# One rotation table, two q and k buffers, one tail transpose, and the second token block's input made during attention: a fused attention and two-layer feed-forward kernel

## The chip, the cores and the metric

One Trainium2 chip, one core. The metric is the device time of one execution in microseconds (us). Each kernel was run several times; the median counts. One more execution was taken by the hardware profiler, and every duration below is from that one.

## The reference, cut to what matters

Attention over 4 batches x 8 heads, 576 tokens, head width 64, in float32, then two feed-forward layers over all 2304 tokens (512 -> 2048 -> 512):

```python
q_rot, k_rot = rotate(q), rotate(k)                 # x1*cos - x2*sin, x1*sin + x2*cos
scores = 1/sqrt(64) * q_rot @ k_rot.T
attn = exp(scores - max); attn /= attn.sum + 1e-9
x = (attn @ v) as [2304, 512]
x = (h - tanh(h)) @ w_out    with h = x @ w_in       # layer one
x = (h * sigmoid(1.702 h)) @ w_out2, h = x @ w_in2   # layer two
```

float32 accuracy is kept by splitting every operand into a high part (rounded to the matmul's format) and a low part (the rest) and adding three products.

## The kernel before, in words

**Work and stages.** Attention works on 16 pairs of heads (`pairs`, 4 batches x 4 pairs). The feed-forward part ("MoE" in the names) works on 6 blocks of 384 tokens x 16 slices of 128 hidden columns x 2 layers: 192 items. An item is an "up" product of 12 matmuls (`up`, L702), an activation on ACT and DVE (`act`), a split on ACT and POOL (`split`, L799 and L801) and a "down" product (`down`, L816).

**A pair in attention.** SP loads q and k of pair n with a swapped copy (`load_qk`, L335; tile `qk`, three buffers). POOL rotates them: two multiplications by the table `tab` (`rope`, L356) and an addition (L358), each over 128x1152 values; ACT rounds the high part (`qk_hi`, L362), POOL takes the low part (`qk_lo`, L400). Four DMAs lay k out twice (`k_twin`, L408, tile `kt`, two buffers) and four lay out q (`q_pair`, L411). Pair 0 goes another way: its q and k come in four pieces with their piece of the table (`load_first`, L341 and L342) and are rotated on DVE (`first_rope`, L372). `v` is split by `v_hi` and `v_lo` (L419). The table holds the q half scaled by 1/8 and the k half unscaled: `tab` is [128, 2, 2, 576].

There are nine units of scores (`UNITS`): four blocks of 128 queries for each head, and one unit (2, 4) that holds the last 64 queries ("tail") of both heads in one 128-row tile. For each unit PE makes scores (L435), DVE the row maximum (L441), ACT the exponentials (L447). PE then transposes the exponentials (`etrans`: L465 the tail unit against the first 512 keys, L472 the others, L476 the last 64 keys of two query blocks, L479 the last 64 keys of one head's tail as a 64x64 transpose with a 64x64 identity, once per head). `evac` copies each transposed bank: ACT the high part (L503), DVE the low part (L501). `pv` multiplies with v (L517); `pv_out` copies to `xt` (L526, L528), `save` writes it to DRAM (L532). Group 1 (`eh`, `el` with 640 columns) holds, per head, 256 query columns and that head's 64 tail columns: head 0 at 0 to 319, head 1 at 320 to 639. Row sums go through `r_add` to `r_save` (one small transpose a pair, L542).

**Feed-forward input.** `x_fetch` (L724, L727) brings a 128-row slice of a block and the reciprocal row sums back from DRAM; `x_split` adds, scales and splits it: three POOL operations (L738, L740, L744) and one ACT copy (L742) for each of four slices. Block 0's tiles live in the pool `xp`, which is open from the start. Block 1's live in the pool `mx`, which is opened only by `close_early`, after the last exponentials (the plan's token `early`). Blocks 0 and 1 go through the first four weight slices one after the other, then the next four and so on (`cuts`). Four weight slices are converted during attention; the other twelve of layer one afterwards, 24 halves of two DVE operations (L282, L284), two POOL (L280, L293) and two ACT operations (L271, L289) each.

**What sets the order.** Every step is an `Op` with a priority, engine costs, what it reads and writes and the buffers it holds. `Plan.order` is a list scheduler in the kernel's own source: it simulates engines and buffers with the hand-written costs, picks among ready operations by priority (`OFF` in units of us from a pair's start, `PER` a pair's length, `T(i)` for items), and its result is fixed as the program order of each engine. So on PE, ACT, DVE, POOL and the SP queue everything runs in that order, and an operation that waits holds up what is behind it. `CAPS` says how many buffers of each tile there are, `XA` and `XB` from what planned time on blocks 0 and 1 may be fetched, `T1` where the items start, and the term 8.6 or 6.3 in `item_ops` how late a "down" stands behind its "up".

Of the kernel before, what the change touches and what calls it, by code (L numbers as in the profile page):

```python
# [40 lines left out]
XA, XB = 218.7, 271.2  # L41
LOOK = {"DVE": 0.15, "ACT": 0.15, "POOL": 0.6, "PE": 0.1, "SP": 2.0}
CAPS = {"qk": 3, "kt": 2, "v": 2, "vw": 2, "e": 7, "ehs": 2, "els": 2, "ehx": 1, "elx": 1, "xt": 3, "mx": 4,
        "sum": 2, "rw": 2, "sp": 2, "st": 2, "cz": 2, "wpa": 4, "wpb": 12, "x": 2, "rb": 1, "rc": 2, "xb0": 1,
        "xb1": 1, "part": 2, "y": 4, "z": 2, "w": 2, "t": 2, "mk": 2, "gh": 2, "gl": 2}

CS, CP, X1 = -0.5, 13.2, 8
CT = (41.4, 75, 90, 105, 120, 135, 150, 159.7)
G = (19.0, 24.0, 17.0)

# [146 lines left out]
def attention_moe_kernel(ctx: ExitStack, tc, qk, v, w1_in, w1_out, w2_in, w2_out, rope_tab, eye, out):  # L197
# [114 lines left out]
    tab = a1.tile([128, 2, 2, S], F32, name="tab")  # L312
# [18 lines left out]
    def load_qk(n, j):  # L331
        b, hp = pairs[n]
        if ("qk", n) not in st:
            st["qk", n] = ae.tile([128, 2, 2, S], F32, tag="qk", name="qk", bufs=3)
        nc.sync.dma_start(out=st["qk", n][:, :, j], in_=qk[b, hp, :, :, j])  # L335

    def load_first(j, c0, c1):
        if ("qk", 0) not in st:
            st["qk", 0] = ae.tile([128, 2, 2, S], F32, tag="qk", name="qk", bufs=3)
# [26 lines left out]
    def first_rope(part, j, c0, c1):  # L366
# [3 lines left out]
        if part < 2:  # L370
            z = (x, y)[part]
            eng.tensor_mul(z, z, tab[:, part, j, c0:c1])  # L372
# [85 lines left out]
    def etrans(n, blk, kk):  # L458
# [14 lines left out]
        else:  # L473
# [3 lines left out]
            if c0 == 2:  # L477
                r = slice(64 * h, 64 * h + 64)
                nc.tensor.transpose(p[0:64, 256:320], st["e", n, (2, 4)][r, 512:576], ident[r, r])  # L479
        st["pe", n, blk, kk] = p  # L480

    def evac(n, blk, kk, low):
# [4 lines left out]
        if c0 == 4:  # L487
            def view(t):
                return t.rearrange("p k (h q) -> p k h q", h=2)[:, 0:4, :, 256:320]
            src, hi, lo = p.rearrange("p k (h q) -> p k h q", h=2), view(eh), view(el)  # L490
        else:
            off = 320 * h if g == 1 else 0
# [3 lines left out]
            else:  # L496
                wd = 320 if c0 == 2 else 256
# [22 lines left out]
    def pv_out(n, h, part):  # L520
        cols, wd = (slice(256, 576), 320) if part == 1 else (slice(0, 256), 256)
        if ("x", n, h) not in st:
            st["x", n, h] = ap.tile([128, S], F32, tag="xt", name="xt", bufs=3)
# [20 lines left out]
    def r_copy(n):  # L544
        rw = st["rw", n] = ap.tile([9, 128], F32, tag="rw", name="rw")
# [20 lines left out]
    for m, a in enumerate(cuts0):  # L566
# [4 lines left out]
        op(-9e3 + m * 20, lambda a=a: load_first(*a), [("SP", 1.26, 1.5 * w)], (), [("q0", m), ("tab", m)], [("qk", 0)], nd=2,  # L571
           dl=(1.9, 0.8 - LAG["SP"]))
    for m, a in enumerate(cuts0):
# [3 lines left out]
        for p in range(2):  # L577
            op(pr + p, lambda p=p, a=a: first_rope(p, *a), [_cost("DVE", d)],
               [("q0", m), ("tab", m)], [("q0", m, p)], [("qk", 0)], port=True)
# [12 lines left out]
    for n in range(NP):  # L592
# [10 lines left out]
        if n:  # L603
            for j in (1, 0):
                op(at("ld") - j * 0.1, bind(load_qk, j), [("SP", 0.62, 1.5)], (), [("qj", n, j)], [Q], G[0] if n == 2 else G[1] if n == 3 else 0.0, dl=HBM)
            for p in range(2):
                op(at(f"r{p}"), bind(rope, p), [_cost("POOL", 2.66)] + alt,
                   [("qj", n, 0), ("qj", n, 1)] + [("tab", m) for m in range(4)], [("rp", n, p)], [Q], port=True)
# [32 lines left out]
        for b, (blk, kk) in enumerate(BLK):  # L641
# [5 lines left out]
            else:  # L647
                us = [IX[h, c0], IX[h, c0 + 1]] + ([IX[2, 4]] if c0 == 2 else [])
                cost, wd = (("PE", 0.6, 0.75), 320) if c0 == 2 else (("PE", 0.25, 0.4), 256)
# [6 lines left out]
            op(at(f"t{b}") + 0.6, bind(evac, blk, kk, False), [_cost("ACT", {512: 0.59, 320: 0.42, 256: 0.37}[wd])],  # L656
               [("t", n, b)], [("th", n, b)], [bt] + ge)
            op(at(f"t{b}") + 1.2, bind(evac, blk, kk, True), [_cost("DVE", {512: 0.683, 320: 0.48, 256: 0.42}[wd])],
               [("t", n, b), ("th", n, b)], [("tl", n, b)], [bt] + ge)
        bi = {x: b for b, x in enumerate(BLK)}  # L660
        for h in range(2):
            for part in range(2):
# [6 lines left out]
                for stage in range(3):  # L669
                    need = [(x, n, bi[blk, stage]) for x in ("th", "tl")]  # L670
                    if part and stage < 2:
                        need += [(x, n, bi[(2, 4), 0]) for x in ("th", "tl")]
# [9 lines left out]
            op(at(f"pv{h}0") + 2, bind(save, h), [("SP", 0.5, 0.78)], [("xt", n, h, 0), ("xt", n, h, 1)], [("xs", n, h)],  # L682
               [("xt", n, h)], dl=(1.2, 0.8))
# [31 lines left out]
    def x_fetch(mo, j, kk):  # L715
# [6 lines left out]
        rb = (pools["mx"] if j else xp).tile([128, TB], F32, tag="rb", name="rb", bufs=2 if j else 1)  # L722
# [113 lines left out]
    T1 = PER * NP + 12  # L836
# [4 lines left out]
    def fetch_ops(mo, j, t, after=0.0):  # L841
        X = (f"xb{j % 2}", mo, j)
        gate = ["early"] if j % 2 else []
        for kk in range(NK):
# [4 lines left out]
            else:  # L849
                bs = {b for b, *_ in pieces(j)}  # L850
                ns = [b * HP + kk for b in bs]
                rb = ("rc" if j else "rb", mo, j, kk)
# [162 lines left out]
```

## Time and profile before, and how to read it

| what | value |
|---|---|
| median of 3 runs | 1111.84 us (1110.89 to 1112.17) |
| the profiled execution | 1112.36 us |
| its span in the profile | 1110.6 us |
| attention | 0 to about 291 us |
| layer one with weight conversion | about 289 to 420 us |
| the rest of both layers | 420 to 1107 us |
| granted TensorE clock | 1.00 in all 40 slices |

PE is the matmul engine, PEld its weight load, DVE, ACT and POOL the vector, scalar and general engines, SP the engine whose queue issues all DMAs here ("SPq" is that queue). L435 is line 435. A row such as "L479 PE ... x32" tells of 32 instructions of that line. In a timeline a bracket says how long the engine had idled before the instruction and what ended the wait. Matmuls are pipelined: a busy time of 0.28 us can stand for 0.12 us of progress, so costs on PE are read from start to start.

### The profile page before, as it was taken

Reading aid. Unit: us, or ns where it says so; the run is one execution under the profiler, and the core shown is the slowest. Engines: PE = TensorE matmul, PEld = TensorE weight load, DVE = VectorE, ACT = ScalarE, POOL = GpSimd, SP = SyncE. Lnnn points to the kernel's source line nnn. Section 1 sums busy time; section 2 is a strip of 40 time slices with the busy share of each in tenths; the row PEclk is TensorE's granted clock in tenths of the full one; section 3 lists DMA queues with packets and bytes.
Section 4 is the critical chain, followed back from the end, with each engine's and each line's share of the span. In section 5 each row is a group of like instructions: output and inputs, shape, how many; then the busy total and the mean of one; then the engine's idle time right before and its main releaser. Section 6 shows DMA issues by size and latency. Waiting matters only on the chain.

```text
span 1110.6 us, 17746 instructions
## 1 busy us (share of the span) xinstructions
PE 1075.9 (97%) x6296; PEld 1008.8 (91%) x6296; DVE 651.8 (59%) x1168; ACT 668.4 (60%) x1474; POOL 597.7 (54%) x502
## 2 busy tenths in 40 slices
PE   4999999999999999999999999999999999999998
PEld 4898999898889989999999999988899999999997
DVE  5999999989769997666667679544212111111110
ACT  4999999988768776556566587654322232232222
POOL 3988888973466667436263267767423232332222
PEclk9999999999999999999999999999999999999999
DMA  9688687764434315203022034443101010010000
GB/s 321 231 295 300 226 302 252 263 220 158 117 124 130 114 58 155 74 1 114 1 79 83 15 101 129 156 133 114 57 1 58 1 57 1 2 42 1 29 1 29
DMA packets 76969, 126.22 MB, mean 114 GB/s; under 512 B 7248, under 2 KB 44368, under 8 KB 76880
## 3 DMA queue, kind: packets, MB, share of 16 engines
q1 hardware_dynamic: 76880, 125.08, 34.2%
q8 instruction: 50, 0.82, 0.3%
q14 instruction: 39, 0.32, 0.1%
HBM read 77.79 MB, written 18.95 MB: 87 GB/s over the span
## 4 chain that ended last, share of the span: by engine, by line
PE 66%; DVE 13%; POOL 6%; ACT 6%; issue 6%; DMA 1%; SPq 1%; POOLq 0%; DVEq 0%; ACTq 0%
PE y L816 27%; PE ps_h L702 27%; PE sp L435 4%; PE ps_o L517 4%; DVE mx L441 3%; PE ps_e L472 3%; DVE el L501 3%; POOL w L293 2%; POOL gl L801 2%; DVE cz L282 2%; DVE cz L284 2%; ACT e L447 2%; POOL cz L280 1%; ACT eh L503 1%; DVE eh L501 1%
## 5 line engine op out<-in xcount | busy, mean ns | idle before, releaser
L702 PE MATMUL ps_h<-xh,w 128*128 128x384 f32 x1536 | 421.2, 336 | 0.6 <-DVE xt L526 0.5
L801 POOL TENSOR_TENSOR gl<-t,gh 128x384 fp32r<-128x384 f32 x192 | 194.7, 1015 | 361.6 <-ACT gh L799 356.8
L702 PEld LDWEIGHTS ps_h<-xh,w 128*128 128x128 f32 x1536 | 280.3, 188 | 5.8 <-DVE t L786 1.1
L702 PE MATMUL ps_h<-xl,w 128*128 128x384 f32 x768 | 257.3, 335 | 0.0
L769 DVE TENSOR_TENSOR t<-t,ps_h 128x384 f32<-128x384 f32 x96 | 53.1, 553 | 280.5 <-ACT t L767 280.5
L816 PE MATMUL y<-gh,w 128*128 128x384 f32 x768 | 195.4, 335 | 2.0 <-ACT gh L799 2.0
L799 ACT CAST gh<-t 128x384 fp32r<-128x384 f32 x192 | 98.8, 514 | 151.1 <-DVE t L792 82.6
L816 PE MATMUL y<-w,gh 128*128 128x512 f32 x576 | 179.4, 392 | 0.0
L767 ACT ACTIVATE t<-ps_h 128x384 f32<-128x384 f32 x96 | 47.1, 491 | 189.1 <-PE ps_h L702 185.7
L702 PEld LDWEIGHTS ps_h<-xl,w 128*128 128x128 f32 x768 | 144.2, 188 | 3.8
L816 PEld LDWEIGHTS y<-gh,w 128*128 128x128 f32 x768 | 138.4, 188 | 3.6 <-ACT gh L799 3.3
L816 PE MATMUL y<-gl,w 128*128 128x384 f32 x384 | 129.2, 337 | 5.3 <-POOL gl L801 5.3
L816 PEld LDWEIGHTS y<-w,gh 128*128 128x128 f32 x576 | 106.7, 188 | 18.2 <-ACT part L825 0.6
L435 PE MATMUL sp<-kt,qt 128*128 128x288 f32 x624 | 115.0, 312 | 2.8 <-ACT e L447 2.5
L816 PE MATMUL y<-w,gl 128*128 128x512 f32 x288 | 114.3, 397 | 1.6 <-POOL gl L801 1.6
L447 ACT ACTIVATE e<-sp,mx 128x576 f32<-128x576 f32 x144 | 107.0, 746 | 14.3 <-DVE mx L441 13.1
L441 DVE TENSOR_REDUCE mx<-sp 128x1 f32<-128x576 f32 x144 | 106.8, 748 | 10.1 <-PE sp L435 9.4
L503 ACT CAST eh<-ps_e 128x512 fp32r<-128x512 f32 (+2 forms) x208 | 102.7, 528 | 8.6 <-PE ps_e L472 6.1
L293 POOL TENSOR_TENSOR w<-cz,w 128x512 fp32r<-128x512 f32 x64 | 82.8, 1294 | 45.6 <-ACT w L289 44.8
L784 DVE SCALAR_TENSOR_TENSOR w<-z,ps_h 128x384 f32<-128x384 f32 x96 | 52.8, 550 | 78.0 <-ACT t L777 76.6
L501 DVE TENSOR_TENSOR el<-ps_e,eh 128x512 fp32r<-128x512 f32 x144 | 95.8, 683 | 4.3 <-ACT eh L503 2.5
L435 PEld LDWEIGHTS sp<-kt,qt 128*128 128x128 f32 x624 | 89.2, 191 | 7.0 <-ACT e L447 5.1
(70 smaller groups left out, 1735.4 us busy)
## 6 DMA issues: line engine op xcount, KB each, us to landing
kt<-qk SPq DMA_DIRECT2D x64, 288.0 KB
qk<-in_qk_dram SPq DMA_DIRECT2D x30, 576.0 KB
st<-in_moe_w_in_dram SPq DMA_DIRECT2D x32, 512.0 KB
st<-in_moe_w_out_dram SPq DMA_DIRECT2D x32, 512.0 KB
qt<-qk SPq DMA_DIRECT2D x64, 144.0 KB
xs<-xt SPq DMA_DIRECT2D x32, 288.0 KB
x<-xs SPq DMA_DIRECT2D x16, 384.0 KB
v<-in_v_dram SPq DMA_DIRECT2D x16, 320.0 KB
```

The costliest lines, as they stand in the source:

```text
L293: nc.gpsimd.tensor_sub(w[:, 2 * self.half + 1], self.cz, w[:, 2 * self.half].bitcast(F32))
L435: nc.tensor.matmul(sp[:, half, 0:HS], lhsT=w, rhs=m[:, half * HS:(half + 1) * HS], start=(o == 0), stop=(o == len(ops) - 1))
L441: nc.vector.tensor_reduce(mx, st["sp", n, i], axis=AX.XY, op=ALU.max, negate=True)
L447: nc.scalar.activation(e.rearrange("p (a b) -> p a b", a=2), st.pop(("sp", n, i)), AF.Exp, bias=st.pop(("mx", n, i)), accum_out=st["sum", ...
L501: nc.vector.tensor_sub(lo, src, hi.bitcast(F32))
L503: nc.scalar.copy(hi, src)
L702: nc.tensor.matmul(p, lhsT=wi[:, a, kk, :], rhs=xx[:, kk, :], start=(o == 0), stop=(o == 11))
L769: nc.vector.tensor_mul(gt[i], gt[i], p)
L784: nc.vector.scalar_tensor_tensor(w, z, G_C[3], p, op0=ALU.mult, op1=ALU.mult)
L799: nc.scalar.copy(gs[i][0], g)
L801: nc.gpsimd.tensor_sub(gs[i][1], g, gs[i][0].bitcast(F32))
L816: nc.tensor.matmul(y, lhsT=lhs, rhs=rhs, start=first and o == 0, stop=last and o == 2)
```

## The change

One rotation table, scaled by 64^-0.25 for q and k alike, [128, 2, 576], loaded in two pieces and read by `rope` as a broadcast over q and k. Two `qk` buffers in place of three, one `rw` buffer in place of two. The last 64 keys of both tails are transposed by one 128-row transpose, in the third step of block (0, 2) alone; the 640 columns of group 1 become head 0 (256), both tails (128), head 1 (256), so head 1's product comes out with its tail in front, its `xt` grows to 640 columns and is saved by two DMAs. Block 1's split tiles move to `xp`, lose the `early` gate, and its fetch may start earlier; so may block 0's. Priorities, some planned costs and `MD` (the lag of a "down") are new, so the planner lays out every engine's order anew.

```diff
-    "ld": -29.13, ... "hi": -6.31, "lo": -5.94, "dk": -13.75,
+    "ld": -35.69, ... "hi": -6.57, "lo": -7.13, "dk": -10.69,
...
-XA, XB = 218.7, 271.2
+XA, XB = 131.7, 200
-CAPS = {"qk": 3, ... "rw": 2,
+CAPS = {"qk": 2, ... "rw": 1,
-CS, CP, X1 = -0.5, 13.2, 8
+CS, CP, X1 = -0.5, 13.2, 30
+MT, MD = 9.7, (8.6, 8.7)
...
-    tab = a1.tile([128, 2, 2, S], F32, name="tab")
+    tab = a1.tile([128, 2, S], F32, name="tab")
...
-            st["qk", n] = ae.tile([128, 2, 2, S], F32, tag="qk", name="qk", bufs=3)
+            st["qk", n] = ae.tile([128, 2, 2, S], F32, tag="qk", name="qk", bufs=2)
...
-        nc.sync.dma_start(out=tab[:, :, j, c0:c1], in_=rope_tab[:, :, j, c0:c1])
         nc.sync.dma_start(out=st["qk", 0][:, :, j, c0:c1], in_=qk[b, hp, :, :, j, c0:c1])
+
+    def load_tab(a):
+        cols = slice(a * HS, a * HS + HS)
+        nc.sync.dma_start(out=tab[:, :, cols], in_=rope_tab[:, :, cols])
...
-            engine().tensor_mul(z, z, tab[:, part])
+            engine().tensor_mul(z, z, tab[:, part:part + 1].to_broadcast([128, 2, S]))
...
-            if c0 == 2:
-                r = slice(64 * h, 64 * h + 64)
-                nc.tensor.transpose(p[0:64, 256:320], st["e", n, (2, 4)][r, 512:576], ident[r, r])
+            if blk == (0, 2):
+                nc.tensor.transpose(p[0:64, 256:384], st["e", n, (2, 4)][:, 512:576], ident)
...
-                wd = 320 if c0 == 2 else 256
+                wd = 384 if blk == (0, 2) else 256
...
-        cols, wd = (slice(256, 576), 320) if part == 1 else (slice(0, 256), 256)
+        cols, wd = (slice(256 + 64 * h, 576 + 64 * h), 320) if part == 1 else (slice(64 * h, 256 + 64 * h), 256)
...
-        nc.sync.dma_start(out=xs[b][hp, h].rearrange("d j t -> (d j) t"), in_=st["x", n, h])
+        dst, x = xs[b][hp, h].rearrange("d j t -> (d j) t"), st["x", n, h]
+        if h == 0:
+            nc.sync.dma_start(out=dst, in_=x[:, 0:S])
+            return
+        nc.sync.dma_start(out=dst[:, 0:512].rearrange("p (a t) -> p a t", a=2),
+                          in_=x.rearrange("p (a t) -> p a t", a=2)[:, :, 64:320])
+        nc.sync.dma_start(out=dst[:, 512:S], in_=x[:, 320:384])
...
-        rb = (pools["mx"] if j else xp).tile([128, TB], F32, tag="rb", name="rb", bufs=2 if j else 1)
+        rb = (pools["mx"] if j > 1 else xp).tile([128, TB], F32, tag="rb", name="rb", bufs=2 if j > 1 else 1)
...
-            pool = pools["mx"] if j % 2 else xp
-            xb[mo, j] = [pool.tile([128, NK, TB], F32R, tag=t, name=t, bufs=1) for t in ("xh", "xl")]
+            xb[mo, j] = [xp.tile([128, NK, TB], F32R, tag=f"{t}{j % 2}", name=t, bufs=1) for t in ("xh", "xl")]
...
-    T1 = PER * NP + 12
+    T1 = PER * NP + MT
...
-        gate = ["early"] if j % 2 else []
...
-            op(t + (8.6, 6.3)[mo] + 0.01 * d, lambda d=d: down(i, d), [("PE", w, w + 0.2)],
+            op(t + MD[mo] + 0.01 * d, lambda d=d: down(i, d), [("PE", w, w + 0.2)],
```

## Rows read from the trace of the kernel before

**Rows 1.** The page: busy us, share of the span and instructions of each engine.

```profile
PE 1075.9 (97%) x6296; PEld 1008.8 (91%) x6296; DVE 651.8 (59%) x1168; ACT 668.4 (60%) x1474; POOL 597.7 (54%) x502
```

**Rows 2.** Busy time by stretch: PE, PEld, DVE, ACT, POOL; clock, DMA share, GB/s.

```profile
0.00:28.00 28.00, 13.31 (x63) 12.21 (x64) 15.99 (x34) 13.54 (x28) 9.50 (x8) 1.00 0.92 322
...
60.00:280.00 220.00, 214.78 (x1620) 198.32 (x1619) 207.27 (x358) 202.71 (x491) 172.12 (x95) 1.00 0.72 247
...
288.00:420.00 132.00, 124.03 (x698) 119.42 (x697) 110.45 (x203) 98.29 (x207) 89.96 (x92) 1.00 0.36 110
...
900.00:1000.00 100.00, 100.00 (x503) 90.58 (x502) 13.30 (x24) 30.12 (x62) 31.82 (x32) 1.00 0.09 28
```

**Rows 3.** Line L542, once a pair: duration min/median/max in ns, first and last start.

```profile
L542 PE MATMUL ps_r<-ident,sum x16: 269/272/278, 40.2 to 287.9; 128*9 128x128 f32 x16
```

**Rows 4.** DMA issues: one piece of the table, count and size.

```profile
tab<-in_rope_dram SPq DMA_DIRECT2D x2, 288.0 KB
```

**Rows 5.** Timeline of the first 13 us: second and third piece's rotation, first matmul.

```profile
7.81 0.82 DVE L372 TENSOR_TENSOR qk<-qk,tab 128x288 f32<-128x288 f32 x2 [0.83 <-DMA qk<-in_qk_dram]
...
10.50 0.82 DVE L372 TENSOR_TENSOR qk<-qk,tab 128x288 f32<-128x288 f32 x2 [1.37 <-DMA qk<-in_qk_dram]
...
12.84 3.50 PE L435 MATMUL sp<-qk,qm 128*128 128x288 f32 x12 [12.84 <-ACT qm L389]
```

**Rows 6.** Timeline of PE: last-key transposes with and without a 64x64 one behind.

```profile
213.82 0.38 PE L476 MATMUL ps_e<-ident,e 128*64 128x128 f32 x2
214.14 0.24 PE L479 MATMUL ps_e<-ident,e 64*64 64x64 f32 x1
214.31 0.66 PE L465 MATMUL ps_e<-ident,e 128*128 128x128 f32 x4
...
216.41 0.38 PE L476 MATMUL ps_e<-ident,e 128*64 128x128 f32 x2
216.54 0.77 PE L435 MATMUL sp<-kt,qt 128*128 128x288 f32 x4
```

**Rows 7.** The chain of waits: first and last 64x64 transpose on it.

```profile
110.73 0.17 PE ps_e L479
...
230.51 0.17 PE ps_e L479
```

**Rows 8.** Groups of instructions by form: tail copies on DVE at two widths.

```profile
L501 DVE TENSOR_TENSOR eh<-ps_e,eh 64x320 fp32r<-64x320 f32 x32 | 15.5, 483 | 2.6 <-ACT eh L503 1.7
L501 DVE TENSOR_TENSOR eh<-ps_e,eh 64x256 fp32r<-64x256 f32 x32 | 13.4, 418 | 2.5 <-ACT eh L503 1.5
```

**Rows 9.** Groups of instructions by form: POOL's rotation and its split of v.

```profile
L356 POOL TENSOR_TENSOR qk<-qk,tab 128x1152 f32<-128x1152 f32 x28 | 74.4, 2666 | 3.2 <-issue 3.0
...
L419 POOL TENSOR_TENSOR vw<-v,vw 128x640 fp32r<-128x640 f32 x16 | 25.4, 1590 | 1.8 <-ACT vw L362 1.3
```

**Rows 10.** Timeline of SP's queue: first and last of eight layout DMAs of a pair.

```profile
172.32 1.32 SPq L408 DMA_DIRECT2D kt<-qk  x2
...
176.32 1.26 SPq L411 DMA_DIRECT2D qt<-qk  x2
```

**Rows 11.** The chain of waits: two DMAs that it waited for to land.

```profile
4.08 6.32 DMA qk<-in_qk_dram
...
285.92 2.55 DMA rb<-rs
```

**Rows 12.** Timeline after attention: POOL's first and last input operation of block 1, DVE.

```profile
287.65 0.99 POOL L738 TENSOR_TENSOR x<-x 128x384 f32<-128x384 f32 x1 [20.79 <-DMA x<-xs]
...
309.76 1.01 POOL L744 TENSOR_TENSOR xl<-x,xh 128x384 fp32r<-128x384 f32 x1
...
311.54 0.69 DVE L282 SCALAR_TENSOR_TENSOR cz<-cp,cz 128x512 int32<-128x512 int32 x1 [6.25 <-POOL cz L280]
```

**Rows 13.** PE's waits: releaser, us in total, times, longest.

```profile
PE y L816 <- POOL gl L801: 6.9, 10, 1.6
```

**Rows 14.** Timeline of PE at the end: the last wait of a "down" product.

```profile
1105.12 0.50 PE L816 MATMUL y<-w,gl 128*128 128x512 f32 x1 [0.31 <-POOL gl L801]
```

More of the change, by code (lines that the diff above doesn't have):

```diff
@@ L371, in first_rope @@
             z = (x, y)[part]
-            eng.tensor_mul(z, z, tab[:, part, j, c0:c1])
+            eng.tensor_mul(z, z, tab[:, part, c0:c1])
         else:
@@ L487, in evac @@
         if c0 == 4:
-            def view(t):
-                return t.rearrange("p k (h q) -> p k h q", h=2)[:, 0:4, :, 256:320]
-            src, hi, lo = p.rearrange("p k (h q) -> p k h q", h=2), view(eh), view(el)
+            src, hi, lo = p, eh[:, 0:4, 256:384], el[:, 0:4, 256:384]
         else:
-            off = 320 * h if g == 1 else 0
+            off = 384 * h if g == 1 else 0
             if kk < 2:
@@ L520, in pv_out @@
     def pv_out(n, h, part):
[L521 removed]
+        cols, wd = (slice(256 + 64 * h, 576 + 64 * h), 320) if part == 1 else (slice(64 * h, 256 + 64 * h), 256)
         if ("x", n, h) not in st:
[L523 removed]
+            st["x", n, h] = ap.tile([128, 640], F32, tag="xt", name="xt", bufs=3)
         o, i = st["x", n, h][:, cols], st.pop(("po", n, h, part))[:, 0:wd]
@@ L544, in r_copy @@
     def r_copy(n):
-        rw = st["rw", n] = ap.tile([9, 128], F32, tag="rw", name="rw")
+        rw = st["rw", n] = ap.tile([9, 128], F32, tag="rw", name="rw", bufs=1)
         p = st.pop(("rt", n))[0:9, 0:128]
@@ L607, in attention_moe_kernel @@
                 op(at(f"r{p}"), bind(rope, p), [_cost("POOL", 2.66)] + alt,
-                   [("qj", n, 0), ("qj", n, 1)] + [("tab", m) for m in range(4)], [("rp", n, p)], [Q], port=True)
+                   [("qj", n, 0), ("qj", n, 1)] + [("tab", 0), ("tab", 1)], [("rp", n, p)], [Q], port=True)
             op(at("r2"), bind(rope, 2), [_cost("POOL", 2.66)] + alt, [("rp", n, 0), ("rp", n, 1)],
@@ L647, in attention_moe_kernel @@
             else:
-                us = [IX[h, c0], IX[h, c0 + 1]] + ([IX[2, 4]] if c0 == 2 else [])
-                cost, wd = (("PE", 0.6, 0.75), 320) if c0 == 2 else (("PE", 0.25, 0.4), 256)
+                us = [IX[h, c0], IX[h, c0 + 1]] + ([IX[2, 4]] if blk == (0, 2) else [])
+                cost, wd = (("PE", 0.335, 0.48), 384) if blk == (0, 2) else (("PE", 0.225, 0.37), 256)
             bt = ("bank", "t", n, blk, kk)
@@ L655, in attention_moe_kernel @@
                [bt] + [("e", n, i) for i in us])
-            op(at(f"t{b}") + 0.6, bind(evac, blk, kk, False), [_cost("ACT", {512: 0.59, 320: 0.42, 256: 0.37}[wd])],
+            op(at(f"t{b}") + 0.6, bind(evac, blk, kk, False), [_cost("ACT", {512: 0.59, 384: 0.48, 256: 0.37}[wd])],
                [("t", n, b)], [("th", n, b)], [bt] + ge)
-            op(at(f"t{b}") + 1.2, bind(evac, blk, kk, True), [_cost("DVE", {512: 0.683, 320: 0.48, 256: 0.42}[wd])],
+            op(at(f"t{b}") + 1.2, bind(evac, blk, kk, True), [_cost("DVE", {512: 0.683, 384: 0.55, 256: 0.42}[wd])],
                [("t", n, b), ("th", n, b)], [("tl", n, b)], [bt] + ge)
@@ L670, in attention_moe_kernel @@
                     need = [(x, n, bi[blk, stage]) for x in ("th", "tl")]
-                    if part and stage < 2:
-                        need += [(x, n, bi[(2, 4), 0]) for x in ("th", "tl")]
+                    if part:
+                        need += [(x, n, bi[((2, 4), 0) if stage < 2 else ((0, 2), 2)]) for x in ("th", "tl")]
                     if stage == 0:
@@ L681, in attention_moe_kernel @@
                    [("po", n, h, part)], [("xt", n, h, part)], [bt, ("xt", n, h)])
-            op(at(f"pv{h}0") + 2, bind(save, h), [("SP", 0.5, 0.78)], [("xt", n, h, 0), ("xt", n, h, 1)], [("xs", n, h)],
-               [("xt", n, h)], dl=(1.2, 0.8))
+            op(at(f"pv{h}0") + 2, bind(save, h), [("SP", 0.5 * (1 + h), 0.78 + 0.2 * h)], [("xt", n, h, 0), ("xt", n, h, 1)],
+               [("xs", n, h)], [("xt", n, h)], nd=1 + h, dl=(1.2, 0.8))
         op(at("rt"), bind(r_add), [_cost("ACT", 0.23)], [("e", n, i) for i in range(9)], [("ra", n)], [("sum", n)])
@@ L851, in fetch_ops @@
                 ns = [b * HP + kk for b in bs]
-                rb = ("rc" if j else "rb", mo, j, kk)
+                rb = ("rc" if j > 1 else "rb", mo, j, kk)
                 op(t + kk * UN - 6, lambda kk=kk: x_fetch(mo, j, kk), [("SP", 1.9 * len(bs), 1.5)],
-                   [("xs", n, h) for n in ns for h in range(2)] + [("rs", n) for n in ns] + (["early"] if j else []), [xt], [xt, rb],
+                   [("xs", n, h) for n in ns for h in range(2)] + [("rs", n) for n in ns] + (["early"] if j > 1 else []), [xt], [xt, rb],
                    after,
@@ L857, in fetch_ops @@
                 uses = [xt, rb]
-                op(t + kk * UN, lambda kk=kk: x_split(mo, j, kk, 0), [_cost("POOL", 1.01)], [xt] + gate, [xt], [xt, rb, X])
+                op(t + kk * UN, lambda kk=kk: x_split(mo, j, kk, 0), [_cost("POOL", 1.01)], [xt], [xt], [xt, rb, X])
                 op(t + kk * UN, lambda kk=kk: x_split(mo, j, kk, 1), [_cost("POOL", 1.01)], [xt], [xt], [xt, rb, X])
-            op(t + kk * UN, lambda kk=kk: x_split(mo, j, kk, 2), [_cost("ACT", 0.51)], [xt] + gate, [("xh", mo, j, kk)],
+            op(t + kk * UN, lambda kk=kk: x_split(mo, j, kk, 2), [_cost("ACT", 0.51)], [xt], [("xh", mo, j, kk)],
                [xt, X])
```

17 lines of the change are left out of this document (10 added, 7 removed), and 10 rows, old and new, of the table OFF.

## The prediction

> **What bounds the kernel now.** I read the page first: PE is busy 97% of the span, no other engine over 60% [rows 1]. That is an average over three stages, so the second view is busy time by stretch [rows 2]. From 900 to 1000 us PE is busy 100.00 of 100 us; the change touches no instruction there, so nothing can be won or lost in the last 690 us except at the very end. From 60 to 280 us (attention) PE is busy 97.6% (214.78 of 220), DVE 94%, ACT 92%, POOL 78%: PE leads, with two engines close behind. From 288 to 420 us PE is idle 132 - 124.03 = 8.0 us. So there are three places to look: the start, where PE makes its first matmul at 12.84 us [rows 5]; attention, 16 pairs of (287.9 - 40.2)/15 = 16.5 us [rows 3]; and the passage into layer one.
>
> The sum is made against the profiled execution, 1112.36 us (span 1110.6 and 1.8 around it), which is 0.5 above the median of the runs, 1111.84.
>
> **The start: the smaller table.** A piece of 128x288 is 288 KB [rows 4]; four pieces of the old table were 1152 KB, the new one is 2 x 288 = 576 KB. Ahead of and with the second k piece, which is the last that the first scores need, the queue carried 1728 KB (three table pieces, three q or k pieces, the identity); now it is 1472 KB. The 256 KB saved (0.26 MB) are worth 0.8 us at the stretch's 322 GB/s [rows 2]. Second view: 576 KB separate the second and the third rotation, 10.50 - 7.81 = 2.69 us [rows 5], so 256 KB are 1.2 us. Everything behind the fourth piece comes 576 KB earlier, 1.8 to 2.7 us. I take **-1.2**, the end of the piece that the first matmul waits for; bounds -0.8 and -2.2. Issues go from eight loads to six and gate nothing: the third pair of loads is issued at about the same place in the queue.
>
> **Attention: the tails' transposes.** Two transposes of L476 followed by ordinary scores take 216.54 - 216.41 = 0.13 us; followed by a 64x64 one they and it take 214.31 - 213.82 = 0.49 [rows 6]. So a 64x64 transpose costs PE 0.36 us, not the 0.07 us that one of L476 takes here. 32 of them are 11.5 us. In their place stand 16 more of the L476 kind at half of 0.13: 1.1 us. PE has **10.4 us** less to do, 0.65 a pair. How much reaches the end? From below: the chain of waits passes through nine of the 32 [rows 7], and 9/32 of 10.4 is 2.9. From above: all 10.4, since PE is the busiest and DVE and ACT leave (220 - 207.27)/13.3 = 1.0 and 1.3 us a pair [rows 2]. The chain is one of several nearly equal ones, so I take the middle of the lower half, **-5**.
>
> What takes the transposes' place next is DVE: row maxima and low parts. Its copies do not shrink: before, both tails went with 320 columns, 2 x 483 ns; now 256 and 384, 418 and, by the same step, 548 ns: 966 both times [rows 8]; ACT's likewise. Head 1's product waits for a copy made earlier in the order than its own: nothing. The tail unit's exponentials are given back earlier: a gain too small to count. One more save DMA a pair, and short rows in it: SP's queue, hidden because the block that reads it comes after attention, and the last pairs' blocks come last. One `rw` buffer: the save before is a pair old, nothing. The broadcast table: no row shows one. From below nothing, since POOL's time goes by elements; from above the slower rate of the split of v, which writes every second element, 1590/640 = 2.48 ns against 2666/1152 = 2.31 [rows 9]: 7% of two operations, 0.4 us a pair, on an engine idle for 22% of the stretch. I take nothing.
>
> **Two q and k buffers.** Pair n+2 now loads into pair n's buffer, so the load waits in SP's queue until the layout DMAs of n have landed; behind it stand v loads, saves and row sums, for which nobody hurries. The turnaround: eight layout DMAs issue in 176.32 + 1.26 - 172.32 = 5.3 us [rows 10], a landing of 2.55 to 6.32 [rows 11], two issues of the load at 5.3/8 each, 1.3, again 2.55 to 6.32: 11.7 to 19.2 us. Meanwhile POOL has the other pair to do: four operations taken at 2.67 each and 1.59 for v, 12.3 us [rows 9]; a pair has 16.5. So POOL waits 0 to 6.9 us a pair and can stand 4.2. I take the short landing, because the queue holds little at that moment but the pair's own layout DMAs: cost **0**, and keep the other end as a rival.
>
> The row says that POOL has 4.2 us a pair to spare. The Trainium skill (Perfetto Trace Analysis, Identifying Performance Opportunities) says that the same gap repeating on the engine that should be saturated can mean too few buffers for the next tile; by that rule taking one away costs what the rival below is priced at, and by the row nothing. No gap that repeats stands on PE now.
>
> **Block 1 earlier.** Now its first POOL operation stands behind a fetch, 20.79 us idle, and its twelve run from 287.65 to 310.8 [rows 12], between the splits of the first items; PE waits 6.9 us in all for those splits (`gl`) [rows 13] and DVE idles 6.25 us before the first conversions [rows 12]. Afterwards twelve POOL and four ACT operations and the fetches, 24 DMAs on SP because the block spans two batches, at 5.3/8 = 0.66 us each [rows 10], lie in attention: POOL's cover is its idle end (the 20.79 us gap holds 12.2). Block 0's move into the middle, where POOL has 48 us to spare in 220. If that cover failed, a rotation would be late by a landing, 2.55 us [rows 11]. Of the 8.0 us that PE idles from 288 to 420 the part after POOL's congestion stays: 24 halves with two DVE operations each are still to convert. Bounds: 0 and -8.0. I take **-4.5**, nearer to the 6.9 of the waits than to nothing, but less, as some of them fall later. What is late next is DVE with conversions.
>
> The new order of all engines has no row. Bounds: it cannot win more than PE's idle 5.2 us in attention nor, as an estimate, lose more than as much; I take 0. The lag of a "down": the last wait of 0.31 us goes [rows 14], **-0.3**, and nothing elsewhere.
>
> **Sum:** -1.2 - 5 - 4.5 - 0.3 = -11.0; 1112.36 becomes 1101.4, and against the median 1100.8.
>
> **Rivals.**
> 1. All of PE's relief arrives: -2.2 - 10.4 - 8.0 - 0.3 = -20.9, **1091**. For: PE at 97.6%. Against: the chain's nine of 32, DVE at 94%.
> 2. DVE and ACT take over at once and attention gains nothing: -1.2 - 4.5 - 0.3, **1106**. For: the long runs of DVE on the chain. Against: 1.0 us a pair of room on DVE.
> 3. **Slower:** two buffers make POOL the bound. Place: the load of n+2 behind the landing of n's layout. It decides from a turnaround of 12.3 + 4.2 = 16.5 us. With both landings at 6.32 a pair takes 19.2, 2.7 more; over 13 pairs +35, less 6 for start and passage: 1141; with five such pairs +13.5 - 6, **1119**. For: DMA share 0.72 in attention [rows 2]. Against: 6.32 us was a landing behind a full start queue. The skill's rule on gaps, above, would be this.
> 4. The change does not do what it says: block 1's input, moved into attention, holds up ACT and POOL there by what it saves after it: start and attention as a wash, **1111**.
>
> **How the numbers follow.** The forecast with its own range of 1096 to 1105 has 0.58, rival 1 0.12, rival 2 0.15, rival 3 0.09, rival 4 0.06. 1093 to 1110 leaves out rival 3, most of rival 4 and the far end of rival 1, some 0.18. 0.2% is 2.2 us, about what a measurement of this kernel can tell from no change. Faster by more than that are the forecast and rivals 1 and 2, less a hundredth for the upper edge: 0.84; the same 0.07; slower 0.09.
>
> **What would show it.** Right: no 64x64 transposes, sixteen more of the 128-row kind; first matmul near 11.6 us; the small transpose of row sums once in some 16.1 us; no POOL operation of block 1's input after attention; PE idle in the 132 us after attention about 3.5 us; the stretch behind unchanged in length. Wrong: POOL idle before a rotation for a load, pair after pair (rival 3); ACT waiting for POOL inside attention (rival 4); a pair still 16.5 us long with DVE on the chain (rival 2).

## The result, and the profile after

The changed kernel takes 1099.61 us (median of four runs, 1097.49 to 1099.76) against 1111.76 us (1110.89 to 1112.17): a ratio of 0.9887, 95% interval 0.987 to 0.9904, so 12.2 us faster. The forecast was 1100.8. The profiled execution took 1099.76 us, its span 1098.0 against 1110.6.

The page after, against [rows 1]:

```profile
PE 1068.8 (97%) x6280; PEld 1007.9 (92%) x6280; DVE 653.6 (60%) x1167; ACT 666.8 (61%) x1473; POOL 602.3 (55%) x504
```

PE has 16 matmuls and 7.1 us of busy time less: 32 of the 64x64 transposes went and 16 of the 128-row kind came. Where the time went is not on this page. Busy time by stretch after, in the stretches of [rows 2]:

```profile
0.00:28.00 28.00, 13.13 (x75) 11.98 (x76) 18.17 (x36) 14.22 (x29) 10.09 (x9) 1.00 0.73 248
60.00:280.00 220.00, 215.19 (x1633) 201.35 (x1631) 207.97 (x358) 206.15 (x503) 192.95 (x111) 1.00 0.76 260
288.00:420.00 132.00, 128.44 (x723) 124.43 (x722) 118.77 (x219) 100.58 (x210) 86.88 (x88) 1.00 0.34 105
900.00:1000.00 100.00, 100.00 (x504) 90.62 (x503) 13.30 (x24) 27.25 (x55) 28.24 (x28) 1.00 0.05 15
```

From 288 to 420 us PE's idle time falls from 8.0 to 132 - 128.44 = 3.6 us, as the prediction said. In attention PE is as busy as before, 215.19 us for 214.78, although it has less to do. The row-sum transpose, once a pair, in the view of its line [rows 3]:

```profile
L549 PE MATMUL ps_r<-ident,sum x16: 269/270/273, 37.4 to 285.3; 128*9 128x128 f32 x16
```

A pair takes (285.3 - 37.4)/15 = 16.53 us on average, for 16.51 before. The 16.1 that the prediction named as its sign did not come.

To see where time is gained, PE's busy time does not help. I added up the columns of the products that both kernels make alike (scores, PV, up and down: 2,121,984 columns in each trace) and took the time at which each trace had done the same amount. The difference is the lead. Each column comes from one profiled execution, and executions of one kernel differ by 1 to 6 us here, so differences of a few tenths say nothing:

```
lead of the changed kernel (us, minus = ahead) when the kernel before stands at
   22    60   120   180   230   260   290   310   360   700   800   900   end of span
 -0.7  -0.1  -0.5  +0.7  -0.2  -2.9  -5.5  -9.3 -10.3 -10.3 -12.1 -12.0  -12.6
```

Nothing is won from 22 to 230 us. The end of attention (230 to 290 us) wins 5.3, the passage into layer one (290 to 360) 4.8 more, the change from layer one to layer two (700 to 900) 1.7, the end 0.6.

The passage, in PE's waits of the whole run after [rows 13], and POOL's last input operation of block 1 [rows 12] with what POOL does next:

```profile
PE y L825 <- POOL gl L810: 2.2, 5, 0.5
```

```profile
279.07 1.00 POOL L753 TENSOR_TENSOR xl<-x,xh 128x384 fp32r<-128x384 f32 x1 [3.06 <-ACT xh L751]
290.07 1.01 POOL L810 TENSOR_TENSOR gl<-t,gh 128x384 fp32r<-128x384 f32 x1 [10.00 <-ACT gh L808]
```

Block 1's input is finished 31 us earlier, and the wait for `gl` falls from 6.9 to 2.2 us; 3.4 us of that fall lie between 280 and 345 us, where none of this wait is left. The chain of waits from 280 to 320 us shows the same: two of its longest pieces before, beside the 2.55 us of [rows 11], and two after:

```profile
281.68 1.62 SPq L724
...
303.06 2.54 DMA rb<-rs
```

```profile
283.35 2.11 PE ps_h L712 x12
...
287.96 4.19 PE ps_h L712 x24
```

Before, no instruction of PE is among the chain's long pieces there: it runs through the fetches of block 1 (L724, L727), their landings and POOL. After, its longest pieces are PE's.

### The profile page after: what moved, and what is told of

It is laid out like the page before. It is cut to its first block, busy times and chain, and to the rows that moved or that the text cites. A ratio compares the mean times of both kernels' runs of the same rounds, so it can differ in the third digit from the quotient of the medians.

```text
span 1098.0 us, 17841 instructions
## 1 busy us (share of the span) xinstructions
PE 1068.8 (97%) x6280; PEld 1007.9 (92%) x6280; DVE 653.6 (60%) x1167; ACT 666.8 (61%) x1473; POOL 602.3 (55%) x504
## 4 chain that ended last, share of the span: by engine, by line
PE 78%; DVE 12%; ACT 4%; POOL 2%; issue 2%; DMA 1%; SPq 0%; ACTq 0%; POOLq 0%; DVEq 0%
PE ps_h L712 32%; PE y L825 32%; PE sp L439 5%; PE ps_o L518 4%; PE ps_e L476 3%; DVE mx L445 2%; DVE el L502 1%; DVE cz L285 1%; DVE cz L283 1%; ACT e L451 1%; DMA qk<-in_qk_dram 1%; DVE eh L502 1%; PE ps_e L480 1%; DVE u L797 1%; DVE u L799 1%
```

## The experiments

Each run was timed against the kernel before on the same chip (medians 1111.88, 1111.74 and 1111.87 us in the three groups). All leads in one table, worked out as above from the profiled execution of each run (e9, whose lead is within 0.4 us of the change's everywhere, is left out):

```
kernel before stands at        60   120   180   230   290   360   700   900
the change                   -0.1  -0.5  +0.7  -0.2  -5.5 -10.3 -10.3 -12.0
e1  square tails             +1.0  +1.6  +3.0  +2.7  -1.4  -6.2  -6.3  -7.9
e2  short lag                +0.5  +0.1  +1.3  +0.1  -5.2 -10.0 -10.1 -10.1
e3  block 1 late             +0.5  +0.1  +0.9  -0.6  -2.6  +0.8  +0.8  -0.8
e4  block 1 late, 3 buffers  +2.9  +4.7  +6.9  +5.7  +4.3  +6.0  +5.3  +3.7
e5  before + new order       +1.1  +2.8  +5.5  +8.4  +7.5  +9.6  +9.0  +9.1
e6  before + two buffers     -0.6  +0.1  +1.4  +0.4  +1.8  +2.5  +2.5  +2.5
e7  before + tails           -0.2  +0.2  -0.4  +1.0  -2.0  +0.7  +0.8  +0.8
e8  change, old order        +0.4  +3.2  +6.6  +6.1  +5.8  +2.3  +2.2  +0.6
e10 before + early block 1   +0.3  +1.0  +2.3  +1.3  +2.1  -2.6  -2.5  -2.5
e11 before + order, 2 buf.   -1.2  +0.1  +2.8  +3.3   0.0  +2.1  +2.1  +2.1
e12 before + one table       +5.7  +7.2  +7.8  +7.4  +7.5  +8.6  +8.7  +8.7
```

**e1, the tails undone in the changed kernel.**

```diff
-            if blk == (0, 2):
-                nc.tensor.transpose(p[0:64, 256:384], st["e", n, (2, 4)][:, 512:576], ident)
+            if c0 == 2:
+                r, o = slice(64 * h, 64 * h + 64), 256 * (1 - h)
+                nc.tensor.transpose(p[0:64, o:o + 64], st["e", n, (2, 4)][r, 512:576], ident[r, r])
```

> The changed kernel with each tail transposed by its own 64x64 transpose again (32 of them instead of 16 of the 128-row kind; layout, buffers, priorities and planned costs stay). My theory: PE is one of three engines that set attention's pace, so 10.4 us more on PE bring about 5: 1104.6 us, and the small transposes of row sums stand 0.3 us further apart per pair from pair 3 on. Rival A, PE alone sets the pace: +10, 1110. Rival B, the transposes were hidden and attention won its time by the new order: within 1.5 of 1099.6.

1103.70 us, ratio 0.9918 (0.9903 to 0.9933): 4.1 slower than the change. The 32 square transposes are back:

```profile
L484 PE MATMUL ps_e<-ident,e x32: 242/243/244, 28.3 to 281.8; 64*64 64x64 f32 x32
```

By the table the distance to the change grows from 1.1 us at 60 to 2.9 at 230 and 4.1 at 290, and stays. The row-sum transposes stand (289.4 - 38.4)/15 = 16.73 us apart, 0.2 more, for the 0.3 expected. So in the changed kernel one transpose for both tails is worth 4.1 us, for the 5 predicted.

**e2, the lag of layer two's "down" undone.** `MD` from (8.6, 8.7) to (8.6, 6.3).

> The changed kernel with the second layer's down lag back at 6.3. Theory: the lag is what won 3 us where layer one passes into layer two and lost about 1.4 after the last up product; so the items behind the passage start 3 us later and the tail is 1.4 shorter, 1101.2 us in all. Rival: the 3 us came from earlier conversions or fetches, not the lag: the items behind the passage stay where they are and only the tail gets shorter, 1098.2.

1101.19 us, ratio 0.9899 (0.9885 to 0.9914): 1.6 slower than the change, as the theory said. The intervals of the two overlap, so the times alone do not show it; the traces do. The lead is that of the change up to 700 and stays at -10.1 where the change goes to -12.0. PE's waits from 690 to 800 us, in this run and before, and busy time of that stretch in this run and after:

```profile
PE y L825 <- POOL gl L810: 1.3, 2, 1.1
...
PE y L816 <- POOL gl L801: 1.3, 2, 1.1
```

```profile
690.00:800.00 110.00, 108.72 (x549) 97.69 (x548) 42.62 (x70) 53.99 (x108) 70.03 (x71) 1.00 0.34 108
```

```profile
690.00:800.00 110.00, 110.00 (x558) 100.12 (x557) 43.44 (x70) 54.80 (x109) 71.29 (x72) 1.00 0.34 109
```

The long lag takes away two waits of PE at the change of layer, 1.3 us in all; after, PE waits for nothing there.

**e3, block 1 late again in the changed kernel.** Its tiles in `mx` behind `early`, its fetches gated, with the old times:

```diff
-XA, XB = 131.7, 200
-CS, CP, X1 = -0.5, 13.2, 30
+XA, XB = 218.7, 271.2
+CS, CP, X1 = -0.5, 13.2, 8
...
+            pool = pools["mx"] if j % 2 else xp
+            xb[mo, j] = [pool.tile([128, NK, TB], F32R, tag=t, name=t, bufs=1) for t in ("xh", "xl")]
```

> The changed kernel with block 1's input again in the late pool, behind the end of attention, and both fetches allowed as late as before. Theory: the passage from attention into layer one loses its 7 us and attention stays: 1106.6. Rival: the twelve POOL and four ACT operations and the fetches inside attention held it up by as much as the passage won; then attention ends 3 to 7 us earlier and the time stays within 3 of 1099.6.

1109.53 us, ratio 0.9977 (0.9967 to 0.9986): 9.9 slower than the change, 2.9 more than expected. Against the change 2.9 us are lost by 290 (-2.6 for -5.5), which the theory did not expect, and 8.2 more by 360 (+0.8 for -10.3). The run also puts block 0's fetch back to its old time; the two were not taken apart. Busy time by stretch of this run in the passage:

```profile
300.00:304.00 4.00, 2.57 (x14) 1.94 (x12) 3.57 (x8) 2.39 (x6) 3.92 (x4) 1.00 0.54 139
304.00:308.00 4.00, 2.76 (x11) 2.77 (x12) 0.34 (x1) 0.93 (x2) 3.92 (x5) 0.78 0.17 35
308.00:312.00 4.00, 3.43 (x11) 2.93 (x11) 1.09 (x2) 1.47 (x3) 3.44 (x5) 0.50 0.40 129
312.00:316.00 4.00, 4.00 (x22) 4.00 (x21) 1.35 (x4) 2.50 (x5) 1.28 (x1) 0.87 0.85 277
```

POOL is full (3.92 of 4), in good part with block 1's input, PE idles, and then the granted clock goes to 0.50, the lower of its two levels. Matmuls of 384 columns, 173 ns apart until then, stand 320 ns apart until 313.1 us. That is 4 x (0.22 + 0.50 + 0.13) = 3.4 us of full-speed time, at most, since PE also waits in it. Whether it is the 2.9 missing in the expectation is not shown: over this run's ten executions the time does not follow the clock (1108.17 us at a mean clock of 0.995, 1107.83 to 1110.65 at 0.998). In the profiled execution of the kernel before the clock stayed at 1.00 here.

**e4, e3 with three q and k buffers.** `bufs=2` to `bufs=3`, `CAPS["qk"]` 3. (Three buffers and an early block 1 together have no room in SBUF, so this was not tried in the full change.)

> As the run with block 1 late, and with three q and k buffers again (both at once, since three buffers and an early block 1 do not fit together). Theory: with two buffers pair 2 and pair 3 load later, and that costs the 3.3 us which the changed kernel lost in pairs 1 to 3: 1103.3, that is 3.3 less than the run with block 1 late and two buffers. Rival: buffers are free, as I predicted, and the loss at the front is a matter of order: within 1 of that run.

1114.20 us, ratio 1.0015 (1.0005 to 1.0026): 4.7 slower than e3 where 3.3 faster was expected. The theory that the missing buffer costs the front of attention falls. In the profiled execution 2.4 us of it are there at 60 us and 6.0 at 180, with the clock low in part of the first 60 us, so its size is not clean; that it has the opposite sign led to e5, e6 and e11.

**e5, the new order alone.** Only the list `OFF` of the change, in the kernel before.

> The kernel before with the list OFF of the changed kernel and nothing else: only the order in which the attention's instructions are issued differs. Basis: counted by the score and PV columns that PE has worked off, the changed kernel is 1.0 us ahead of the kernel before at 22 us and 0.9 us behind it at 182 us, while the run with the two square tails is there another 1.5 us further behind than at the start; so something of the change costs about 3.4 us by then. Theory (the new order costs it): 1111.9 + 3.4 = 1115.3 us, 1113.5 to 1117. Rival (the loss of the third q and k buffer costs it, the order costs nothing): 1112 us, 1111 to 1113. Second rival (the order is better by itself): under 1110.5.

1121.21 us, ratio 1.0087 (1.0072 to 1.0102): 9.5 slower, nearly three times the theory's price. The loss grows from 60 to 230 us, 7.3 us in all. The granted clock was at its lower level from 193 to 197 us, which can make up 1.7 of it.

**e6, two buffers alone.** `bufs=3` to `bufs=2`, `CAPS["qk"]` 2, in the kernel before.

> The kernel before with two q and k buffers in place of three and nothing else, its own order kept. Theory (the order costs the 3.4 us, the buffers nothing): 1112 us, 1111 to 1113. Rival (the buffers cost it): 1111.9 + 3.4 = 1115.3 us, 1113.5 to 1117. The rival of the prediction that makes POOL the bound: 1119 to 1141 us.

1114.91 us, ratio 1.0034 (1.0021 to 1.0047): 3.2 slower, inside the rival's range. So neither theory of this pair of runs was whole: with the old order the missing buffer costs 3.2 us, and the new order costs more still where there are three.

**e7, the tails alone** (layout, evictions, saves, planned costs and one `rw` buffer with them).

> The kernel before with the tails of the changed kernel alone: one transpose for both tails of a stage, the 128-column layout, its evictions, its PV columns, its three saves in place of two, its costs in the planner and one rw buffer; three q and k buffers, two tables, block 1 late and the old order stay. The prediction: -5.0, 1106.9 us. Theory after the run with the square tails (their progress drifts apart by 3.1 us from the first pair to the last): 1108.8 us, 1107.5 to 1110. Rival (PE's relief is taken up by the next engine): 1111 to 1113 us.

1113.36 us, ratio 1.0018 (1.0009 to 1.0028): 1.6 slower; all three expectations miss, the last rival's by least. Yet attention did win: the lead is -2.0 at 290. It is lost by 360. POOL's last parts of block 1's input in this run:

```profile
307.97 1.00 POOL L747 TENSOR_TENSOR xl<-x,xh 128x384 fp32r<-128x384 f32 x1
312.24 0.99 POOL L747 TENSOR_TENSOR xl<-x,xh 128x384 fp32r<-128x384 f32 x1
```

The last one starts at 312.24, for 309.76 before [rows 12]; in e3, with a lead of 2.6, at 309.10. The plan puts block 1's input behind the last exponential, which PE's lead had not moved: it starts at 282.15 us here and 282.00 before. In the eight traces with block 1 late its input ends 27.4 to 31.1 us after the last exponential starts, while that start lies anywhere from 281.4 to 289.9. It is not the fetch that waits for the exponential: the first one starts at 281.77 here and 281.68 before, right behind a save, and in e6 and e12 four us before the exponential, and the input ends no sooner behind it. Part of what holds the input is ACT's order, which has the copy `xh` behind activations of the first items. In the kernel before POOL stands 4.53 us for it:

```profile
294.27 1.02 POOL L744 TENSOR_TENSOR xl<-x,xh 128x384 fp32r<-128x384 f32 x1 [4.53 <-ACT xh L742]
```

**e8, the change with the old order.** The whole change but its list `OFF`.

> The changed kernel with the list OFF of the kernel before, loads included. Theory (the new order costs 3.4 us): 1099.6 - 3.4 = 1096.2 us, 1094.5 to 1098. Rival (the order belongs to two buffers and one transpose, and is better there): 1101 us or more, because loads would be asked for at times at which no buffer is free and the operations behind them stand in POOL's order. Second rival (order is worth nothing either way): 1099 to 1100.5 us.

1112.32 us, ratio 1.0001 (0.9992 to 1.001): all 12.2 us of the change are gone, in attention (lead +5.8 at 290 for -5.5). The theory's 1096 falls; the first rival's "1101 or more" holds, with another reason than loads that find no buffer. Busy time from 60 to 230 us in this run and after:

```profile
60.00:230.00 170.00, 160.40 (x1207) 148.29 (x1206) 156.69 (x269) 157.95 (x373) 145.98 (x77) 1.00 0.74 258
```

```profile
60.00:230.00 170.00, 165.29 (x1249) 154.08 (x1248) 161.31 (x276) 159.79 (x389) 156.68 (x84) 1.00 0.78 269
```

POOL's timeline through one pair, in this run and after (rotations L360, their sum L362, v's low part L423, the keys' low part L404):

```profile
75.41 5.30 POOL L360 TENSOR_TENSOR qk<-qk,tab 128x1152 f32<-128x1152 f32 x2
80.79 2.67 POOL L362 TENSOR_TENSOR qk<-qk 128x1152 f32<-128x1152 f32 x1
84.88 1.57 POOL L423 TENSOR_TENSOR vw<-v,vw 128x640 fp32r<-128x640 f32 x1 [1.42 <-PE ps_e L480]
90.01 2.66 POOL L404 TENSOR_TENSOR qk<-qk 128x1152 fp32r<-128x1152 f32 x1 [3.56 <-ACT qk L366]
92.62 5.32 POOL L360 TENSOR_TENSOR qk<-qk,tab 128x1152 f32<-128x1152 f32 x2
```

```profile
74.26 5.29 POOL L360 TENSOR_TENSOR qk<-qk,tab 128x1152 f32<-128x1152 f32 x2
79.64 2.66 POOL L362 TENSOR_TENSOR qk<-qk 128x1152 f32<-128x1152 f32 x1
...
84.80 2.65 POOL L404 TENSOR_TENSOR qk<-qk 128x1152 fp32r<-128x1152 f32 x1
89.09 2.67 POOL L360 TENSOR_TENSOR qk<-qk,tab 128x1152 f32<-128x1152 f32 x1 [1.64 <-DMA qk<-in_qk_dram]
```

In both the next pair's rotation follows the low part. From the first rotation to the end of the low part it is 92.67 - 75.41 = 17.3 us with the old order and 87.45 - 74.26 = 13.2 with the new, because POOL stands 3.56 us for ACT's rounding (L366) that is late in ACT's order: it starts at 88.78, 5.3 us behind the sum, for 83.49 and 1.2 us after. From 60 to 230 us POOL waits for this rounding 8.6 us in six places, after 3.2 in three. That the round sets the pair's period is argued from its length and not shown by a run: the row-sum transposes, at 36.5 us first and 296.6 last, are 17.3 us apart on average.

The tails and the order belong together, too. With the old order the lead at 290 is +2.1 in e10 and +5.8 here, where the tails, their planned costs and the items' new times are added; with the new order the tails win 4.1 (e1).

**e9, a shorter end.** The last four items' "down" with a lag of 6.3 in the changed kernel. A first reading of the trace after, by the start of each item's split, had been that the lag wins 3.3 at the change of layer and costs 1.4 at the end.

> The changed kernel, but the down products of the last four items become due 6.3 us after their item in place of 8.7. Theory (the run with the short lag: the long lag won 3.3 us at the change of layer and cost 1.4 us behind the last up product, and the two can be had apart): 1099.6 - 1.4 = 1098.2 us. Rival (the end is bound by the last item's own chain whatever the order): 1099.6 us.

1100.07 us, ratio 0.9894 (0.9879 to 0.9908), against 1099.61: nothing won, as the rival said. The 1.4 us were then no time: the same products stand behind the last "up" in place of before it. No version that I ran beats the change.

**e10, block 1 early with the old order.** The kernel before with two buffers and one table, which make the room, and block 1 (and block 0) fetched early; square tails, old order.

> The kernel before with two q and k buffers, one table (which make the room) and block 1's input in its own pool during attention; the old order, the square tails and the old lag and start of the items stay. Basis: the run with two buffers alone (1114.9), which is 2.5 us behind the kernel before from item 16 on. Theory (with block 1 late the passage is bound by the last exponential plus some 28 us, so that early input takes 7 us or more off it): 1114.9 - 7 = 1108 us, 1106 to 1109.5. The prediction's term of -4.5: 1110.4 us. The prediction's rival (block 1's work in attention gives it back): 1114 us or more.

1110.30 us, ratio 0.9987 (0.9977 to 0.9996): 4.6 less than two buffers alone. The lead goes from +2.1 at 290 to -2.6 at 360: 4.7 us in the passage, where the prediction said 4.5 and the theory 7. (Two buffers alone lose 0.7 there, so against e6 early input is worth 5.4.)

**e11, two buffers and the new order,** in the kernel before.

> The kernel before with two q and k buffers and the list OFF of the changed kernel: the fourth corner of the square of which the new order alone (1121.2) and two buffers alone (1114.9) are two. If the two costs add up: 1111.7 + 9.5 + 3.2 = 1124.4 us. Theory (an order fits the buffers for which its loads were set, and the new order with its loads 6.6 us earlier is good with two): 1115 us or less, 1111 to 1116. Second theory (the order fits the whole changed kernel, tails and inputs too, not the buffers): 1118 to 1123 us.

1114.08 us, ratio 1.0020 (1.0010 to 1.0029). If the two costs added up it would be 1124.4; it is 10.3 less. The new order costs 9.5 us with three buffers; with two it costs nothing (0.8 less, within the two intervals). It wins nothing with two either: by the table order and buffers together lose 3.3 us by 230 and have them back at 290. Two buffers make the new order harmless; what makes it good is in the rest of the change.

**e12, one table alone.**

> The kernel before with one rotation table and nothing else: two DMAs of the table in place of four, q and k of the first pair as before. The prediction's term: -1.2, 1110.5 us. Theory (the first matmul starts about 1 us earlier, but with block 1 late the passage waits for the last exponential, which stands where it stood, since attention is held by DVE and ACT as much as by PE): 1111.0 to 1112.5 us. Rival (the rotation with a broadcast table costs more on DVE or POOL): over 1113 us.

1118.84 us, ratio 1.0062 (1.0043 to 1.0081): 7.0 slower, the rival's number but not its cause: in the profiled execution, which took 1121.07, 5.7 of the 8.7 us lost are there at 60 us, and a rotation takes 7.83/3 = 2.61 us in the rows below, no more than the 2.67 of [rows 9]. POOL's timeline of the start, in this run and before (L361 and L358 the sum, L359 and L356 rotations, L400 the low part of pair 1):

```profile
18.61 2.64 POOL L361 TENSOR_TENSOR qk<-qk 128x1152 f32<-128x1152 f32 x1
21.21 1.57 POOL L422 TENSOR_TENSOR vw<-v,vw 128x640 fp32r<-128x640 f32 x1
22.74 7.83 POOL L359 TENSOR_TENSOR qk<-qk,tab 128x1152 f32<-128x1152 f32 x3
```

```profile
18.70 2.62 POOL L358 TENSOR_TENSOR qk<-qk 128x1152 f32<-128x1152 f32 x1 [18.26 <-DVE qk L356]
21.28 1.58 POOL L419 TENSOR_TENSOR vw<-v,vw 128x640 fp32r<-128x640 f32 x1
22.82 2.65 POOL L400 TENSOR_TENSOR qk<-qk 128x1152 fp32r<-128x1152 f32 x1
```

Both stand alike at 22.8 us. There the kernel before takes the low part of pair 1, which PE needs next; here POOL makes three rotations for later pairs, 7.83 us. The low part could not have been taken at that point, for ACT rounds pair 1's high part only at 26.92 us, in place of right behind the sum. Then DVE makes the low part, which takes it 3.67 us for POOL's 2.65, and PE waits for it. ACT in this run and before, DVE in this run:

```profile
26.92 1.16 ACT L365 CAST qk<-qk 128x1152 fp32r<-128x1152 f32 x1
...
21.36 1.16 ACT L362 CAST qk<-qk 128x1152 fp32r<-128x1152 f32 x1 [0.23 <-POOL qk L358]
...
28.11 3.67 DVE L403 TENSOR_TENSOR qk<-qk 128x1152 fp32r<-128x1152 f32 x1 [0.36 <-ACT qk L365]
```

Busy time by stretch of this run:

```profile
28.00:32.00 4.00, 1.49 (x13) 1.28 (x11) 3.89 (x2) 0.45 (x2) 3.92 (x2) 1.00 0.00 0
32.00:36.00 4.00, 2.63 (x12) 2.09 (x13) 1.87 (x3) 3.33 (x8) 3.50 (x2) 0.75 0.65 243
```

An earlier load makes the planner lay out ACT's and POOL's queues the wrong way round, and the low clock behind the pause (0.75 in the mean of 32 to 36 us) adds to it. Two buffers prevent the three rotations: e10 has one table with two buffers, and its lead at 60 us is +0.3, for +5.7 here. One table and two buffers were not tried without e10's early block 1.

## Why the prediction was right, and where it was not

The total was right to 1.2 us, and the terms of the tails and of the passage came out near their size. But the part without which nothing is won was a term that I had put at zero.

**The start, -1.2.** The first matmul starts at 11.39 us for 12.84 [rows 5]. Over the runs it is 11.39 to 12.00 with one table and 12.05 to 12.84 with two, 0.7 apart in the mean, just under the lower bound. By 60 us the lead is -0.1: whatever the start won is taken back there. One table alone even costs 7.0 us.

**Attention, -5.** Start and attention together were predicted at -6.2; the lead at 290 is -5.5. The tails' part is -4.1 in the changed kernel (e1), in the lower half of the bounds 2.9 and 10.4, where the prediction put it. It comes at 0.2 us a pair. The whole change shows none of it up to 230 us, since other parts lose as much there: two buffers and the new order together lose 3.3 by 230 and nothing by 290 (e11), and -4.1 on top of that is most of the -5.5. Nor does the gain belong to the transposes alone: in the kernel before they win 2.0 us in attention, and the passage takes that back (e7). The items' earlier start in the plan (`MT`) was not undone by itself.

**Two buffers, 0.** Alone they cost 3.2 us (e6). POOL can become the bound, as rival 3 said: in e8 its round from rotation to low part is 17.3 us, over the 16.5 from which that was said to decide. But the place is another: the round is long by a wait for ACT inside it, not by slow landings. In the changed kernel the load stands on the chain of waits from 140 to 220 us once, with the rotation of pair 12 behind it:

```profile
181.31 8.39 DMA qk<-in_qk_dram
...
190.10 5.27 POOL qk L360 x2
```

The load had been issued behind a fetch of block 0 (L734, L737). A cost of zero holds in attention as a whole, but only with the new order (e11: lead 0.0 at 290).

**The passage, -4.5.** -4.8 in the change, -4.7 in e10. What the prediction did not see is that with block 1 late its input ends some 28 us behind the last exponential, so that no lead of PE in attention passes it: e7 loses 2.7 us there, e3 3.4 (the low clock in it), e11 2.1. Early input is worth 4.8 us and also lets the rest through; with the 2.9 us before 290 that is why undoing it costs 9.9.

**The new order, 0.** This step failed. It was said to have no row, and bounded by PE's idle 5.2 us in attention on either side. Without it the change is worth nothing (e8, 1112.32); in the kernel before it costs 9.5 (e5). The upper bound was taken from the idle time of the kernel before, but what the new order saves is idle time that the rest of the change would make: from 60 to 230 us PE idles 170 - 160.40 = 9.6 us in e8 and 4.7 after. The lower bound had no ground in the rows. That the total came out all the same is luck: the zeros for order and buffers are each wrong alone (+9.5, +3.2) and hold only together, by 290 us in e11.

Busy time of PE is also a poor measure of what it won. Attention in two stretches before, and the second one after (the first one after stands under e8):

```profile
60.00:230.00 170.00, 166.15 (x1257) 153.96 (x1256) 160.35 (x276) 159.28 (x384) 149.22 (x75) 1.00 0.76 263
230.00:290.00 60.00, 57.34 (x424) 51.69 (x423) 53.59 (x95) 50.11 (x124) 24.92 (x23) 1.00 0.55 180
```

```profile
230.00:290.00 60.00, 59.67 (x449) 56.41 (x448) 54.91 (x97) 53.74 (x131) 36.34 (x28) 1.00 0.69 226
```

The lead gains 0.1 us in the first stretch and 5.3 in the second. The Trainium skill (Perfetto Trace Analysis, Identifying the Most-Contended Engine) says that matmul busy time is not a good measure of how close a kernel is to its limit, because pipelined matmuls look smaller in the trace, and names the matmul work done in a stretch and the time busy with weight loads as better ones. The trace agrees: PEld gains 0.1 and 4.7 us in the two stretches, PE's busy time -0.9 and 2.3.

**Nothing elsewhere, -0.3 at the end.** The lead still grows by 1.7 us at the change of layer and 0.6 at the end. e2 shows the cause of the first: the longer lag of layer two's "down" removes two waits of 1.3 us in all. The prediction had read 900 to 1000 us, where PE never idles, for all of the last 690 us.

So the sum of -11.0 came out as -5.5 - 4.8 - 1.7 - 0.6 = -12.6 of span, but the parts are no sum: table, buffers, tails and order, each alone in the kernel before, cost 7.0, 3.2, 1.6 and 9.5 us. Which entries of the list make the new order good was not taken apart, nor which part of the change besides two buffers it needs (the tails are one, by e1, e8 and e10), and why e4 is so slow was not settled.

## What to carry to other kernels

Where a planner or a hand-written list fixes each engine's order, buffers, loads and order are one part: testing one of them alone can show the wrong sign, and a change of buffers is judged only with an order made for it. To find where a change wins, compare when both traces have done the same amount of the work they share, not how busy the engine is. And ask of each gain what the next stage waits for: if that is another event than the one moved, here block 1's input behind the last exponential, the gain ends there.

## What the hardware showed that I had not expected

TensorE's clock. In e3 PE was busy 2.57 and 2.76 of 4 us at 300 to 308 us, with one pause of 2.5 us, and the granted clock fell to 0.50 from 308 to 312, the lower level. The kernel before, with 2.63 and 2.41 of 4 us busy from 304 to 312, kept 1.00, and so did e7 with 1.54 of 4 from 304 to 308 and one pause of 2.1 us. Pauses of much the same size cost up to 3.4 us or nothing.

At the start the clock column does not tell the pace. Busy time by stretch of the kernel before, and its score matmuls in the groups by form, the first two lines from 13 to 25 us and the last from 30 to 60:

```profile
13.00:25.00 12.00, 10.16 (x40) 9.11 (x41) 8.63 (x13) 8.31 (x18) 6.30 (x3) 1.00 1.01 372
```

```profile
L435 PE MATMUL sp<-qk,qm 128*128 128x288 f32 x24 | 7.1, 469 | 13.5 <-ACT qm L389 12.8 <-ACT e L447 0.7
L435 PE MATMUL sp<-kt,qt 128*128 128x288 f32 x6 | 1.8, 466 | 0.0
...
L435 PE MATMUL sp<-kt,qt 128*128 128x288 f32 x74 | 13.5, 311 | 0.6 <-ACT e L447 0.6
```

The column says 1.00, yet these matmuls take 466 to 469 ns each before 25 us and 311 ns from 30 to 60 us, the same operands (`kt`, `qt`) among them. Started one behind the other, they stand 240 ns apart until 25.0 us and 134 ns from 25.4 on, not far from the ratio of the two levels. In the changed kernel the step comes between 20.0 and 20.6 us. The clock's records in the two traces begin only with the step, at 25.3 and 20.4 us, and the column counts a time without a record as 1.00: the 1.00 of the first slice of the kernel before is no measurement.
